# Holding back SyncE's transfers in a block-sparse attention + MLP kernel: each one waits for the landing of the fifth last

## Chip, core and metric

The kernel runs on one core of a Trainium2 chip. The metric is device time in microseconds (us), the median of several executions. Engine names are those of the profile: PE is the matmul engine and PEld its weight loads, DVE is VectorE, ACT is ScalarE, POOL is GpSimd, SP is SyncE, which here does nothing but register arithmetic, waiting and issuing DMA transfers.

## What is computed

```
scores = q @ k^T / sqrt(64)            # 4 batches, 8 heads, 768 positions, fp32
mask: block 32x32; own and neighbour blocks, first and last block row/column,
      and 3 sampled key blocks per query block (given at run time)
attn   = softmax(where(mask, scores, -1e9)) ;  x = attn @ v
x -> 3072 tokens x 512
h = x @ w_in (512 x 2048) ; r = max(h, 0) ; out = (s*r*r + b) @ w_out (2048 x 512)
```

The weights `w_in` and `w_out` come as float64 and are decoded on the chip into two fp32r halves each.

## The kernel before

Two stages share one program. The attention takes the first 260 us or so, the MLP the rest. The attention is cut into "slots": 44 sparse ones (one query block of two batches, all heads; streams A, B and C take turns) and 8 dense ones (first and last block rows). In each sparse slot PE makes the scores (L925), DVE takes the maximum (L942), ACT the exponential (L954), PE transposes (L982), DVE or ACT copies to SBUF (L993, L995), and PE multiplies by the values (L1034, 64 recorded matmuls and 64 weight loads per slot, some from tile `vA`, some from `vB`). Then the result is scaled (L1040), transposed back (L1046), copied by ACT into one of four `xst` buffers (L1051) and written to DRAM (`spill`, L1058 and L1062), from where the MLP reads it (`xload`, L392).

The transfers of the attention and who issues them:

- SP: the keys `kt` (`load_k`, L689 and L692), the queries of dense slots (`load_q`, L706), the three sampled value blocks of each slot (`sampled_v`, L847, three per sparse slot, and L844 for the last block), the whole first window of a stream (`window_v`, L753), the spills, the raw weights of the first `EARLY_W` = 6 weight tiles (`load` in `decode_f64`, L59 and L62), and the loads of x for the MLP's first two groups (L392).
- POOL: the queries of sparse slots (`load_q`, L706) and the next block of each window (`window_v`, L753). POOL also copies keys into `kk` (L864, L875).

The order of the instructions on every engine is written out by a planner (class `Plan`), which runs at build time with a cost for each operation. Its model of SP lets eight transfers be under way:

```
QUEUE = 8
...
sent.append(dma + 850.0)
free[e] = max(free[e], sent[-self.QUEUE])
```

The framework turns the order into queues with semaphores. SP's transfers go through eight landing semaphores in turn, so that a transfer also waits until the eighth last one of SP has landed. An instruction that waits on SP holds up all that stands behind it on SP. The instructions of every engine are themselves brought in by DMA; the profile counts these packets under "instruction".

Of the kernel before, what the change touches and what calls it, by code (L numbers as in the profile page):

```python
# [12 lines left out]
I32 = mybir.dt.int32  # L13
# [23 lines left out]
    return x if x < 2 ** 31 else x - 2 ** 32  # L37


def decode_f64(nc, n, src, top, most, raw_of, mag_of, low_of, hi_of, lo_of):  # L40

    box = {}

    def get(k, fn):
        if k not in box:
            box[k] = fn()  # L50
        return box[k]

    def raw():
        return get("raw", raw_of)

    def load(m=0, parts=1):
        if len(src.shape) == 3:
            a = src.shape[1] // parts
            nc.sync.dma_start(out=raw().rearrange("p (a c) -> p a c", a=src.shape[1])[:, m * a:(m + 1) * a], in_=src.bitcast(I32)[:, m * a:(m + 1) * a])  # L59
        else:  # L60
            a = 2 * n // parts
            nc.sync.dma_start(out=raw()[:, m * a:(m + 1) * a], in_=src.bitcast(I32)[:, m * a:(m + 1) * a])  # L62

    def word(k):
        return raw().rearrange("p (n two) -> p n two", two=2)[:, :, k]

    def mag(t=I32):
        return get("mag", mag_of).bitcast(t)

    def low(t=F32):  # L70
        return get("low", low_of).bitcast(t)

    def hi():
        return get("hi", hi_of)

    A, V = nc.scalar, nc.vector
    return load, [

        ("v", lambda: V.tensor_scalar(out=mag(), in0=word(1), scalar1=0x7FFFFE00, scalar2=None, op0=ALU.bitwise_and), ()),

        ("v", lambda: V.tensor_scalar(out=low(I32), in0=word(1), scalar1=0x1FF, scalar2=None, op0=ALU.bitwise_and), ()),
        ("v", lambda: V.scalar_tensor_tensor(out=low(), in0=low(I32), scalar=2.0 ** 32, in1=word(0).bitcast(U32), op0=ALU.mult, op1=ALU.add), (1,)),  # L82
        ("a", lambda: A.activation(word(1).bitcast(F32), word(1).bitcast(F32), AF.Sign), (0, 1)),

        ("a", lambda: A.activation(mag(F32), mag(), AF.Relu, scale=-8.0, bias=top), (0,)),
        ("a", lambda: A.activation(mag(), mag(F32), AF.Relu, scale=-1.0, bias=most), (4,)),
        ("v", lambda: V.tensor_tensor(out=hi(), in0=mag(F32), in1=word(1).bitcast(F32), op=ALU.mult), (3, 5)),  # L87
        ("v", lambda: V.tensor_scalar(out=mag(), in0=hi().bitcast(I32), scalar1=_i32(0xFF800000), scalar2=None, op0=ALU.bitwise_and), (6,)),  # L88
        ("v", lambda: V.scalar_tensor_tensor(out=lo_of(), in0=low(), scalar=2.0 ** -52, in1=mag(F32), op0=ALU.mult, op1=ALU.mult), (2, 7)),  # L89
    ]  # L90
# [116 lines left out]
def kernel(  # L207
# [16 lines left out]
    nc = tc.nc  # L224
# [4 lines left out]
    NB = 24  # L229
    BLK = 32  # L230
    NPAIR = 4
    NSP = 5
    NSL = 3
# [4 lines left out]
    NM = 12  # L238
    KPS = (4, 24)
    NBC, NCK = 3, 8  # L240
    EARLY_W = 6
# [13 lines left out]
    b_top = cpool.tile([P, 1], F32, name="b_top")  # L255
    nc.gpsimd.memset(b_top, F32_MOST + F64_SHIFT)
    b_most = cpool.tile([P, 1], F32, name="b_most")
    nc.gpsimd.memset(b_most, F32_MOST)
    xd = dpool.tile([B // 2, 2, P, NM, 2, NPAIR, BLK], F32, name="xd")
    wod = dpool.tile([4, P, 2 * DM], F32, name="wod")  # L260

    kp = ctx.enter_context(tc.tile_pool(name="kp", bufs=2))

    def kbig(q, name):
# [2 lines left out]
    NW = NCC * P  # L269
# [103 lines left out]
    def decode(which, f, n):  # L373
        tail = (lambda: scratch("kraw", 2 * NW, f"raw_{which}{f}").bitcast(I32), *parts(n))
        if which == "i":
            src, view = w_in[:, f * P:(f + 1) * P].rearrange("(c p) n -> p c n", p=P), win
        else:
            src, view = w_out[f * P:(f + 1) * P, :], wout
        return decode_f64(nc, NW, src, b_top, b_most, *tail, lambda: view(f, 0), lambda: view(f, 1))


    xsp, xraw, kg_pairs = {}, {}, {}
# [6 lines left out]

    def xload(g, c2, dst=None):  # L390
        t = scratch("kraw", 2 * HALF, f"xraw{g}_{c2}") if dst is None else dst
        nc.sync.dma_start(out=t.rearrange("p (t y) -> p t y", t=NM), in_=xd[g // 4, g % 2, :, :, g // 2 % 2, 2 * c2:2 * c2 + 2, :].rearrange("p t c n -> p t (c n)"))  # L392
        xraw[(g, c2)] = t

    def xsplit(g, c, part=None):
# [259 lines left out]
    with ExitStack() as es:  # L655
# [12 lines left out]
        for w in T["ORD"].split():  # L668
            if w[1] == "D":
                slots.append(("d", "abcd".index(w[0]), int(w[2]), 0))  # L670
            else:
                r = "ABC".index(w[1])
# [8 lines left out]
        kts = {}  # L681


        def load_k(e, a, part):
            if e not in kts:
                kts[e] = kbig(e, f"kt{e}").bitcast(F32)
            rows = slice(part * NB // KPS[e], (part + 1) * NB // KPS[e])
            if a is None:
                nc.sync.dma_start(out=kts[e][:, rows].rearrange("p n a c -> p n (a c)"),  # L689
                                  in_=k_blk[rows, :, 2 * e:2 * e + 2, :].rearrange("n p a c -> p n (a c)"))  # L690
            else:
                nc.sync.dma_start(out=kts[e][:, rows, a], in_=k_blk[rows, :, 2 * e + a, :].rearrange("n p c -> p n c"))  # L692

        qts = {}

# [4 lines left out]
        def load_q(key, a, par):  # L700
            kind, e, t = key
            if key not in qts:
                qts[key] = qp.tile([P, 2, NPAIR, P], F32, tag="qr", name=f"qr{e}_{t}{kind}")
            rows, b = slice(par * D, (par + 1) * D), 2 * e + a
            src = q_dup[b, t, rows, par::2, :] if kind == "s" and t < NSP else q_edge[b, int(kind == "d"), rows, par::2, :]
            (nc.gpsimd if kind == "s" else nc.sync).dma_start(out=qts[key][rows, a], in_=src)  # L706

        vbox = {}

# [5 lines left out]
        def window_values(r):  # L715
            value_tiles()
            return vbox["A"][:, r]
# [16 lines left out]
        def block_rows(e, j, n=1):  # L734

            return v[2 * e:2 * e + 2, j * BLK:(j + n) * BLK, :].rearrange("a r d -> r a d")
# [11 lines left out]
        def window_v(i, entire, m):  # L748

            _, e, k, r = slots[i]  # L750
            rr = [*runs(k, entire), *[(0, NSL, 1)] * entire]
            j, p, n = rr[m]
            (nc.sync if entire else nc.gpsimd).dma_start(out=window_values(r)[p * BLK:(p + n) * BLK], in_=block_rows(e, j, n))  # L753


        ident = pers.tile([P, P], F32, name="ident")
# [18 lines left out]
        box = {}  # L775

        def load_sampled():
            nc.sync.dma_start(
                out=sbi,
                in_=sampled.bitcast(I32).rearrange("a b -> (a b)").rearrange("(o n) -> o n", o=1)  # L780
                .broadcast_to([P, 2 * NB * NSL]))
# [54 lines left out]
        def sampled_v(i, a):  # L836


            _, e, k, r = slots[i]
            row = ring_row("v", i)  # L840
            vt = sampled_values(row)
            if a == 0 and holds["v"].get(row) != e:
                holds["v"][row] = e
                nc.sync.dma_start(out=vt[NSL * BLK:], in_=block_rows(e, NB - 1))  # L844
            src = v[2 * e:2 * e + 2].rearrange("a (n e) d -> n e a d", e=BLK)
            j = block_register(mybir.EngineType.SP, k, r, a)
            nc.sync.dma_start(out=vt[a * BLK:(a + 1) * BLK], in_=src[bass.ds(j, 1)].rearrange("o e a d -> (o e) a d"))  # L847

        def keys_tile():
            if "kk" not in vbox:  # L850
# [202 lines left out]
        def spill(i):  # L1053
            kind, b, k, _ = slots[i]
            xst = xst_of.pop(i)
            if kind == "s":
                hf, m = divmod(k - 1, NM)
                nc.sync.dma_start(out=xd[b, hf, :, m].rearrange("p a c n -> p a (c n)"), in_=xst)  # L1058
                return
            x = k  # L1060
            for m in range(2):
                nc.sync.dma_start(out=xd[b // 2, 1, :, NM - 2 + m, b % 2, 2 * x:2 * x + 2, :],  # L1062
                                  in_=xst.rearrange("p x (a m n) -> p (x a) m n", a=2, m=2)[:, :, m, :])


# [60 lines left out]
        for i, (kind, e, k, r) in enumerate(slots):  # L1126
# [28 lines left out]
            else:  # L1155
                prev = before.get(r)
                entire = k == STREAMS[r]
# [16 lines left out]
                vt = [("vg", "vA"), ("vg", "vB")]  # L1174
                for m in range(len(runs(k, entire)) + entire):
                    n = [*[x for _, _, x in runs(k, entire)], 1][m]
# [8 lines left out]
                lo, n = T["K1"]  # L1185
# [7 lines left out]
            for c in range(2):  # L1193
# [4 lines left out]
                o = op("p", cost[0], u, lambda i=i, c=c: scores(i, c), cols=col[0], deps=deps,  # L1198
                       alloc=banks if new else [], use=[*s_use, *([] if new else banks)])
# [4 lines left out]
            for j in range(nu):  # L1204
                n, ms_ = u + j, []
# [6 lines left out]
                for g in range(ng):  # L1212
                    top = g == 0 and j == 0
# [7 lines left out]
                    else:  # L1221
                        n0, both = n - 1, [half, o_e]
                    o = op("p", 470, u, lambda n=n0, g=g: transposes(n, g), both, cols=1024, alloc=[("B", ("t", n0, g))],
                           use=[("P", (y, g)) for y in range(n0, n + 1)])
# [21 lines left out]
            for j in range(nu):  # L1246
                pts = [("pt", (u + j // 2 * 2, 0))]
                o = op("p", cost[2], u, lambda i=i, j=j: av(i, j), cols=col[2],
                       deps=[*evs[j], *av_deps],
                       alloc=[] if j else [("o", i)],  # L1250
                       use=[*av_use, *pts] + ([("o", i)] if j else []))
# [11 lines left out]
            if k % NBC == 1:  # L1263
                left = sum(sl[0] == "s" and sl[1] == e and sl[2] % NBC == 1 for sl in slots[i + 1:])
                done[e] = done.get(e, 0) + 1
                for b in (2 * e, 2 * e + 1):
                    g = (k - 1) // NBC // (NCK // 2)
# [266 lines left out]
```

## Time and profile before

| | us |
|---|---|
| median of three runs | 784.31 |
| lowest, highest | 782.02, 786.36 |
| profiled execution, device time | 786.43 |
| its span, first to last instruction | 784.7 |
| granted TensorE clock, mean | 0.984 |

The profiled execution is one run, 2.1 us above the median. Its span leaves 1.7 us of the device time outside. Positions in the text ("at 84 us") count from the start of the span. "Landing" is the time from a transfer's issue until its semaphore tells that all data is there. In the chain of work that ended last, "issue" is time in which the engine waited for nothing that the profile shows.

### The profile page before, as it was taken

Reading aid. Unit: us, or ns where it says so; the run is one execution under the profiler, and the core shown is the slowest. Engines: PE = TensorE matmul, PEld = TensorE weight load, DVE = VectorE, ACT = ScalarE, POOL = GpSimd, SP = SyncE. Lnnn points to the kernel's source line nnn. Section 1 sums busy time; section 2 is a strip of 40 time slices with the busy share of each in tenths; the row PEclk is TensorE's granted clock in tenths of the full one; section 3 lists DMA queues with packets and bytes.
Section 4 is the critical chain, followed back from the end, with each engine's and each line's share of the span. In section 5 each row is a group of like instructions: output and inputs, shape, how many; then the busy total and the mean of one; then the engine's idle time right before and its main releaser. Section 6 shows DMA issues by size and latency. Waiting matters only on the chain.

```text
span 784.7 us, 21376 instructions
## 1 busy us (share of the span) xinstructions
PE 734.5 (94%) x8032; PEld 622.3 (79%) x8032; DVE 583.5 (74%) x1436; ACT 472.3 (60%) x1141; POOL 270.4 (34%) x435
## 2 busy tenths in 40 slices
PE   7888689799898999999979999999999999999997
PEld 6566567466566899998768988898999898989996
DVE  3856467788886699998998678687668778666652
ACT  3866466787776687778764334475544467434543
POOL 5836447336641223220423223232232223222321
PEclk9999899999999999999999999999999999999999
DMA  8979689757872444543632421125000022000002
GB/s 249 244 205 239 179 222 252 177 152 197 228 200 88 119 134 142 180 134 119 154 118 66 122 76 61 48 61 162 1 1 1 1 60 82 2 1 0 1 1 80
DMA packets 100167, 89.41 MB, mean 114 GB/s; under 512 B 50464, under 2 KB 79776, under 8 KB 100064
## 3 DMA queue, kind: packets, MB, share of 16 engines
q1 hardware_dynamic: 95936, 76.78, 34.4%
q0 software_dynamic: 4128, 11.28, 5.5%
q8 instruction: 63, 1.03, 0.6%
q14 instruction: 40, 0.33, 0.1%
HBM read 69.15 MB, written 14.68 MB: 107 GB/s over the span
## 4 chain that ended last, share of the span: by engine, by line
PE 65%; DVE 20%; issue 6%; ACT 5%; DMA 2%; SPq 1%; POOL 1%; POOLq 0%; ACTq 0%; DVEq 0%
PE m L611 20%; PE o L475 8%; PE o L476 8%; PE o L474 8%; PE s L925 5%; PE xs L1034 5%; PE t L982 4%; DVE ptile L942 2%; PE od L1024 2%; DVE wkhp L88 2%; PE t L980 2%; PE s L903 1%; PE xs L1046 1%; DVE win L89 1%; DVE wklp L82 1%
## 5 line engine op out<-in xcount | busy, mean ns | idle before, releaser
L453 POOL TENSOR_TENSOR hid<-hid,hid 128x384 fp32r<-128x384 f32 x122 | 134.8, 1106 | 359.6 <-ACT hid L629 261.6
L628 ACT ACTIVATE hid<-hid,sb_b,sb_s 128x384 f32<-128x384 f32 x96 | 68.0, 708 | 151.6 <-DVE hid L622 151.5
L954 ACT ACTIVATE ptile<-ptile,nm 128x256 f32<-128x256 f32 (+1 forms) x208 | 107.0, 517 | 43.2 <-DVE nm L942 43.1
L942 DVE CUSTOM_DVE_ANT_1 ptile<-s,mt 128x256 f32<-128x256 f32 x176 | 64.3, 421 | 29.5 <-PE s L925 28.7
L611 PE MATMUL m<-wout,win 128*128 128x384 f32 x264 | 63.1, 342 | 4.6 <-ACT xrest L1427 4.6
L475 PE MATMUL o<-woutr,hid 128*128 128x512 f32 x168 | 66.4, 396 | 0.7 <-DVE woutr L89 0.7
L476 PE MATMUL o<-woutr,hid 128*128 128x512 f32 x168 | 66.5, 396 | 0.0
L474 PE MATMUL o<-woutr,hid 128*128 128x512 f32 x168 | 65.5, 390 | 0.5 <-DVE woutr L87 0.5
L611 PE MATMUL m<-xp,wop 128*128 128x384 f32 x288 | 58.7, 338 | 0.0
L1034 PEld LDWEIGHTS xs<-vA,pt 128*32 128x32 f32 x1696 | 35.7, 112 | 27.2 <-issue 7.8
L475 PE MATMUL o<-win,hid 128*128 128x512 f32 x144 | 56.8, 394 | 0.0
L622 DVE SCALAR_TENSOR_TENSOR hid<-hid 128x384 f32<-128x384 f32 x96 | 54.0, 563 | 3.3
L611 PE MATMUL m<-xp,win 128*128 128x384 f32 x288 | 54.8, 337 | 1.1 <-DVE sum L1436 0.8
L1034 PE MATMUL xs<-vA,pt 128*32 128x64 f32 x1696 | 47.9, 227 | 7.6 <-issue 3.0
L611 PEld LDWEIGHTS m<-xp,win 128*128 128x128 f32 x288 | 51.0, 188 | 3.7 <-ACT ob L480 1.1
L629 ACT CAST hid<-hid 128x384 fp32r<-128x384 f32 x96 | 49.3, 514 | 7.6 <-ACT hid L628 0.4
L611 PEld LDWEIGHTS m<-wout,win 128*128 128x128 f32 x264 | 48.0, 190 | 7.3 <-ACT xrest L1427 5.5
L611 PEld LDWEIGHTS m<-xp,wop 128*128 128x128 f32 x288 | 52.0, 190 | 2.1
L982 PE MATMUL t<-ident,ptile 128*128 128x128 f32 x352 | 51.6, 290 | 0.9 <-issue 0.8
L875 POOL COPY kk<-kt 128x256 f32 x132 | 50.9, 419 | 0.0
L476 PE MATMUL o<-win,hid 128*128 128x512 f32 x126 | 50.0, 397 | 0.3 <-POOL hid L453 0.3
L621 DVE TENSOR_TENSOR hid<-m,xrest 128x384 f32<-128x384 f32 x48 | 26.5, 551 | 31.0 <-issue 26.4
(184 smaller groups left out, 1867.5 us busy)
## 6 DMA issues: line engine op xcount, KB each, us to landing
vB<-in_v_dram SPq DMA_DIRECT2D x113, 128.0 KB, 4.0
raw_o<-in_w_out_dram SPq DMA_DIRECT2D x14, 512.0 KB, 3.3
raw_i<-in_w_in_dram SPq DMA_DIRECT2D x12, 512.0 KB, 3.8
xd<-xst SPq DMA_DIRECT2D x44, 128.0 KB, 3.9
out_dram<-ob SPq DMA_DIRECT2D x20, 256.0 KB, 2.0
vA<-in_v_dram SPq DMA_DIRECT2D x39, 128.0 KB, 4.1
vA<-in_v_dram POOLq DMA_DIRECT2D x38, 128.0 KB, 3.7
sum<-xd SPq DMA_DIRECT2D x12, 384.0 KB, 4.2
```

What stands on the lines that cost most here:

```text
L453: (eng or nc.vector).tensor_tensor(out=htile(5 + i % 3), in0=t, in1=gh.bitcast(F32), op=ALU.subtract)
L474: nc.tensor.matmul(acc, gh[:, tsl], wout(f, 0), start=first, stop=False)
L475: nc.tensor.matmul(acc, gh[:, tsl], wout(f, 1), start=False, stop=False)
L476: nc.tensor.matmul(acc, gl[:, tsl], wout(f, 0), start=False, stop=last)
L611: nc.tensor.matmul(to, w_, x_, start=(c == 0 and k == 0), stop=(c == 1 and k == 2))
L622: vec.scalar_tensor_tensor(out=t, in0=t, scalar=0.0, in1=t, op0=ALU.max, op1=ALU.mult)
L628: nc.scalar.activation(t, t, AF.Identity, bias=sb_b, scale=sb_s)
L875: nc.gpsimd.tensor_copy(flat(kg[:, a:a + 1]), flat(kts[e][:, bass.ds(j, 1)]))
L942: nc.vector.tensor_tensor_reduce(out=pt, in0=sp, in1=msk, scale=-scale, scalar=FMAX if g == 0 else nm[:, 0:1], op0=ALU.add, op1=ALU.min, a ...
L954: nc.scalar.activation(pt[:, :w], pt[:, :w], AF.Exp, bias=nms[n][:, last:last + 1], scale=-1.0, accum_out=dns[i][:, g, j:j + 1])
L982: nc.tensor.transpose(tp[:, (2 * j + c) * P:(2 * j + c + 1) * P], src[:, c * P:(c + 1) * P], ident)
L1034: nc.tensor.matmul(xs[quads[pair]], pt[:, c, quads[pair]], vt[:, a, col:col + D], start=(j == 0 and c == 0), stop=(c == 1), tile_position= ...
```

## The change

A function `send` takes the place of SP's own issue for the transfers of the attention. It issues the transfer on SP as before, and from the 21st on it adds a dependency: the transfer waits until the fifth last one sent in this way has landed. Which engine issues what, and the planner with its order, stay as they are. POOL's transfers are not held. The raw weights from the seventh tile on, and all later transfers of the MLP, go out as before; so do the two tiny loads of `s` and `b`.

```
+    sent, LEAD, OUT = [], 20, 5
+
+    def send(**kw):
+        ins = nc.sync.dma_start(**kw)
+        if len(sent) >= LEAD:
+            tc.add_manual_dep(ins.ins, sent[-OUT].ins.name, mybir.DependencyInfo(mybir.DependencyClass.Sync, mybir.DependencyReason.DATA))
+        sent.append(ins)
...
-def decode_f64(nc, n, src, top, most, raw_of, mag_of, low_of, hi_of, lo_of):
+def decode_f64(nc, issue, n, src, top, most, raw_of, mag_of, low_of, hi_of, lo_of):
...
-            nc.sync.dma_start(out=raw()[:, m * a:(m + 1) * a], in_=src.bitcast(I32)[:, m * a:(m + 1) * a])
+            issue(out=raw()[:, m * a:(m + 1) * a], in_=src.bitcast(I32)[:, m * a:(m + 1) * a])
...
-        return decode_f64(nc, NW, src, b_top, b_most, *tail, lambda: view(f, 0), lambda: view(f, 1))
+        return decode_f64(nc, send if n < EARLY_W else nc.sync.dma_start, NW, src, b_top, b_most, *tail, lambda: view(f, 0), lambda: view(f, 1))
...
-            (nc.gpsimd if kind == "s" else nc.sync).dma_start(out=qts[key][rows, a], in_=src)
+            (nc.gpsimd.dma_start if kind == "s" else send)(out=qts[key][rows, a], in_=src)
...
-            (nc.sync if entire else nc.gpsimd).dma_start(out=window_values(r)[p * BLK:(p + n) * BLK], in_=block_rows(e, j, n))
+            (send if entire else nc.gpsimd.dma_start)(out=window_values(r)[p * BLK:(p + n) * BLK], in_=block_rows(e, j, n))
...
-            nc.sync.dma_start(out=vt[a * BLK:(a + 1) * BLK], in_=src[bass.ds(j, 1)].rearrange("o e a d -> (o e) a d"))
+            send(out=vt[a * BLK:(a + 1) * BLK], in_=src[bass.ds(j, 1)].rearrange("o e a d -> (o e) a d"))
```

In the same way `nc.sync.dma_start` becomes `send` in `xload` (for the first two groups), `load_k`, `load_sampled`, the L844 load of `sampled_v`, and both forms of `spill`.

## Rows read from the trace of the kernel before

**Rows 1.** The page: span, engines; queue of instructions (packets, MB, share of the engines).
```profile
span 784.7 us, 21376 instructions
...
PE 734.5 (94%) x8032; PEld 622.3 (79%) x8032; DVE 583.5 (74%) x1436; ACT 472.3 (60%) x1141; POOL 270.4 (34%) x435
...
q8 instruction: 63, 1.03, 0.6%
```

**Rows 2.** Chain that ended last: start, us, what; the "issue" pieces.
```profile
34.49 1.16 issue
...
45.36 1.76 issue
...
69.46 0.56 issue
...
74.29 1.52 issue
...
79.69 0.42 issue
...
83.95 5.47 issue
...
129.76 1.03 issue
...
143.07 1.87 issue
```

**Rows 3.** Stretches: length, busy us of PE to POOL, PEclk, DMA share, GB/s.
```profile
66.00:93.00 27.00, 19.03 (x527) 13.82 (x527) 15.06 (x60) 14.73 (x51) 14.35 (x32) 0.88 0.83 224
75.81:79.69 3.88, 3.88 (x127) 2.93 (x127) 2.11 (x7) 1.73 (x7) 2.75 (x6) 1.00 1.02 255
80.12:83.95 3.83, 3.83 (x127) 2.87 (x126) 3.11 (x13) 2.76 (x10) 3.12 (x8) 1.00 0.88 241
```

**Rows 4.** SP's L847, L1058, L689, then POOL's L753, L706, from 66 to 88 us.
```profile
L847 SPq DMA_DIRECT2D vB<-in_v_dram x10: 316/330/1123, 66.6 to 79.8; - x10
...
L847 SPq DMA_DIRECT2D vA<-in_v_dram x3: 342/342/484, 81.4 to 83.1; - x3
...
DMA to landing us min/median/max: 4.5/6.3/7.9
...
L1058 SPq DMA_DIRECT2D xd<-xst x5: 349/364/373, 65.7 to 82.5; - x5
...
L689 SPq DMA_DIRECT2D kt<-in_k_blk_dram x9: 334/422/1528, 67.0 to 86.1; - x9
...
L753 POOL DMA_DIRECT2D vA<-in_v_dram x6: 536/550/550, 67.4 to 84.3; - x6
...
L706 POOL DMA_DIRECT2D qr_3s<-in_q_dup_dram x4: 615/623/629, 69.1 to 73.1; - x4
```

**Rows 5.** Landing of L847's transfers, first from 40 to 66 us, then 118 to 147.
```profile
DMA to landing us min/median/max: 2.1/3.7/5.9
...
DMA to landing us min/median/max: 2.4/5.1/6.4
```

**Rows 6.** Stretches as in 3: after the longest stop, 118 to 150, after the attention.
```profile
89.42:93.20 3.78, 3.78 (x42) 2.86 (x50) 1.37 (x4) 0.86 (x2) 0.00 (x0) 0.50 0.05 16
118.00:150.00 32.00, 28.58 (x613) 20.31 (x615) 24.29 (x85) 21.91 (x67) 16.56 (x37) 0.96 0.91 235
262.00:385.00 123.00, 120.72 (x602) 108.34 (x601) 113.33 (x188) 96.95 (x175) 27.25 (x24) 1.00 0.49 146
```

**Rows 7.** L1034's matmuls up to 110.35 us; then L847's transfers up to 100.2 us.
```profile
L1034 PE MATMUL xs<-vA,pt x640: 216/219/244, 30.2 to 108.0; 128*32 128x64 f32 x160
...
L1034 PE MATMUL xs<-vB,pt x384: 216/219/316, 38.7 to 103.3; 128*32 128x64 f32 x192
...
L847 SPq DMA_DIRECT2D vB<-in_v_dram x41: 316/326/1179, 21.4 to 100.1; - x41
...
L847 SPq DMA_DIRECT2D vA<-in_v_dram x12: 316/340/484, 15.7 to 83.1; - x12
```

More of the change, by code (lines that the diff above doesn't have):

```diff
@@ L58, in load @@
             a = src.shape[1] // parts
-            nc.sync.dma_start(out=raw().rearrange("p (a c) -> p a c", a=src.shape[1])[:, m * a:(m + 1) * a], in_=src.bitcast(I32)[:, m * a:(m + 1) * a])
+            issue(out=raw().rearrange("p (a c) -> p a c", a=src.shape[1])[:, m * a:(m + 1) * a], in_=src.bitcast(I32)[:, m * a:(m + 1) * a])
         else:
             a = 2 * n // parts
-            nc.sync.dma_start(out=raw()[:, m * a:(m + 1) * a], in_=src.bitcast(I32)[:, m * a:(m + 1) * a])
+            issue(out=raw()[:, m * a:(m + 1) * a], in_=src.bitcast(I32)[:, m * a:(m + 1) * a])
     def word(k):
@@ L391, in xload @@
         t = scratch("kraw", 2 * HALF, f"xraw{g}_{c2}") if dst is None else dst
-        nc.sync.dma_start(out=t.rearrange("p (t y) -> p t y", t=NM), in_=xd[g // 4, g % 2, :, :, g // 2 % 2, 2 * c2:2 * c2 + 2, :].rearrange("p t c n -> p t (c n)"))
+        (send if g < 2 and dst is None else nc.sync.dma_start)(out=t.rearrange("p (t y) -> p t y", t=NM), in_=xd[g // 4, g % 2, :, :, g // 2 % 2, 2 * c2:2 * c2 + 2, :].rearrange("p t c n -> p t (c n)"))
         xraw[(g, c2)] = t
@@ L688, in load_k @@
             if a is None:
-                nc.sync.dma_start(out=kts[e][:, rows].rearrange("p n a c -> p n (a c)"),
+                send(out=kts[e][:, rows].rearrange("p n a c -> p n (a c)"),
                                   in_=k_blk[rows, :, 2 * e:2 * e + 2, :].rearrange("n p a c -> p n (a c)"))
             else:
-                nc.sync.dma_start(out=kts[e][:, rows, a], in_=k_blk[rows, :, 2 * e + a, :].rearrange("n p c -> p n c"))
+                send(out=kts[e][:, rows, a], in_=k_blk[rows, :, 2 * e + a, :].rearrange("n p c -> p n c"))
         qts = {}
@@ L777, in load_sampled @@
         def load_sampled():
-            nc.sync.dma_start(
+            send(
                 out=sbi,
@@ L843, in sampled_v @@
                 holds["v"][row] = e
-                nc.sync.dma_start(out=vt[NSL * BLK:], in_=block_rows(e, NB - 1))
+                send(out=vt[NSL * BLK:], in_=block_rows(e, NB - 1))
             src = v[2 * e:2 * e + 2].rearrange("a (n e) d -> n e a d", e=BLK)
             j = block_register(mybir.EngineType.SP, k, r, a)
-            nc.sync.dma_start(out=vt[a * BLK:(a + 1) * BLK], in_=src[bass.ds(j, 1)].rearrange("o e a d -> (o e) a d"))
+            send(out=vt[a * BLK:(a + 1) * BLK], in_=src[bass.ds(j, 1)].rearrange("o e a d -> (o e) a d"))
         def keys_tile():
@@ L1057, in spill @@
                 hf, m = divmod(k - 1, NM)
-                nc.sync.dma_start(out=xd[b, hf, :, m].rearrange("p a c n -> p a (c n)"), in_=xst)
+                send(out=xd[b, hf, :, m].rearrange("p a c n -> p a (c n)"), in_=xst)
                 return
@@ L1061, in spill @@
             for m in range(2):
-                nc.sync.dma_start(out=xd[b // 2, 1, :, NM - 2 + m, b % 2, 2 * x:2 * x + 2, :],
+                send(out=xd[b // 2, 1, :, NM - 2 + m, b % 2, 2 * x:2 * x + 2, :],
                                   in_=xst.rearrange("p x (a m n) -> p (x a) m n", a=2, m=2)[:, :, m, :])
```

## The prediction

> **What bounds the kernel now.** I read the page first. PE is busy 94% of the span [rows 1], so only a change that gives PE time back, or takes some, moves the end. The second view is the chain of work that ended last, cut to the attention, the only part that the diff touches. Most of its pieces are PE's, but between them stand pieces called "issue", in which PE waits for nothing that the profile shows: eight of them, from 0.42 to 5.47 us, in [rows 2], 13.8 us in sum. What are they? The stretches between two of them answer it. From the end of the piece at 74.29 to the next, and from there to the one after, PE ran 127 matmuls and 126 or 127 weight loads each time [rows 3], wherever in a block of work that ended (the stop at 83.95 is between two matmuls of L1034). The page has 63 packets of instructions on one queue, 1.03 MB, so 16.4 KB each, and PE has 8032 + 8032 instructions [rows 1], 255 for each packet. So PE stops where one packet of its own instructions is used up and the next is not there: an instruction fetch, which is a DMA, comes late.
>
> The third view is the landing of the data transfers in the same stretch. From 66 to 88 us SP's L847 takes 6.3 us in the median to land [rows 4], from 40 to 66 us 3.7 us [rows 5], and the DMA engines are 83% busy [rows 3]. PE uses up a packet in 3.8 to 3.9 us [rows 3]. A fetch that lands as late as the data beside it then holds PE. The four stops from 66 to 93 us (0.56, 1.52, 0.42, 5.47) sum to 7.97 us, just the 27.00 - 19.03 us in which PE is idle there [rows 2, 3].
>
> **How deep SP's queue is.** Transfers under way are their number times their landing time over the stretch. From 66 to 88 us SP issues 13 of L847, 5 of L1058 and 9 of L689, 27 in 22 us [rows 4]; with 6.3 us for each (the one median shown) that is 7.7 under way, about the eight that the framework allows. POOL issues 6 of L753 and two groups of four of L706 (one of the two is shown) [rows 4], 14; with the same landing, 4.0 under way. So the rule of five binds here, and takes 11.7 under way to 9.0. From 40 to 66 us SP's L847 lands in 3.7 us, and the rule binds in bursts only.
>
> **The change part by part.**
>
> *The wait itself* is SP's alone. Behind a waiting transfer stand the next transfers with their register arithmetic, and the spills. For them wait PE (sampled values), POOL (keys) and ACT (a free `xst`, of which there are four). What covers the delay is that sampled values come early. The first 16 sparse slots are 16 x 64 = 1024 matmuls of L1034, and these (640 + 384) had run by 110.35 us. The 17th slot needs 51 transfers of L847; 53 had been issued by 100.2 us [rows 7]. Even with the longest landing of [rows 4], 7.9 us, the data is there by 108.1 us, 2.3 us ahead; worked out in the same way from each slot's own landing, the slack of all 44 slots is 8.3 us (this one) or more. Cost taken: 0. If the cover is gone, each us beyond it is a us of PE's.
>
> *Does the rule slow the flow of data?* With 4.9 us to land (below), five under way are 1.02 transfers per us, and 27 in 22 us are 1.23. The flow of SP would be 17% lower, and in a 22 us burst the last transfer 22 x (1.23/1.02 - 1) = 4.5 us late, less than the 8.3 us. If instead the DMA engines, 83% busy, stay as busy, POOL's transfers and the fetches just go first and nothing is late. Bounds: 0 and 4.5 us of delay, all under the slack; I take 0 for PE.
>
> *Earlier fetches.* If landing follows the number under way, it falls by 1 - 9.0/11.7 = 23%: from 6.3 to 4.9 us, 1.4 us less. If only SP's own queue counts, by 1 - 5/7.7 = 35%, 2.2 us less. From 66 to 93 us the stops of 0.56 and 0.42 go, and 1.52 and 5.47 lose 1.4 each: 3.8 us (with 2.2 us: 4.7). From 118 to 150 us L847 lands in 5.1 us [rows 5], 23% are 1.2 us: 1.03 goes, 1.87 loses 1.2, 2.2 us. The stop at 34.49 loses 0.9, 23% of the 3.7 us of the stretch behind it. The one at 45.36 stands where landing is short, and keeps its 1.76. Sum 6.9 us.
>
> Not all of it reaches the end. From 66 to 93 us the chain holds PE and "issue" alone, so 3.8 counts in full. From 118 to 150 us DVE is busy 24.3 of 32 us [rows 6] and shares the chain; I count half of 2.2, and half of 0.9 at 34.49: 1.5. From 5.3 I take 0.8 off, since a fetch that now falls outside a burst may then fall into one (a 1.76 us stop with short landings shows that chance has a part). **Value: 4.5 us**, between 0 (fetches do not follow the queue) and 6.9, with 4.7 in place of 3.8 some 8 us.
>
> *The clock.* After the stop of 5.47 us PE ran at 0.50 of its clock (1.2 in place of 2.4 GHz) from 89.42 to 93.20, 3.78 us of work [rows 6] that takes 1.9 us at full clock. If the stop gets short enough, 1.9 us more come back. At 4.1 us it would still be the longest of all; I take 0, and put 1.9 into the range.
>
> *What the gain meets later.* After the attention DVE decodes weights and PE runs the MLP, with DVE busy 113 and PE 121 of 123 us [rows 6]: full engines that start as much earlier as the attention ends earlier. Nothing of the diff acts there, since the loads from the seventh weight tile on are not held.
>
> **Sum.** 786.43 - 4.5 = 781.9 us for the profiled execution, which is 2.1 us above the median of 784.31. Off the median: 779.8 us, 0.57% less. About 0.5% (3.9 us) is what a measurement of this kernel can tell from no change.
>
> **Rivals.**
>
> *No change to be seen (784 us).* A fetch on its own queue may not care how many of SP's transfers wait in theirs. For it: the stop of 1.76 us at 45.36 in a stretch of short landings, and stops of 0.42 and 5.47 us one after the other in the same deep burst. Against it: three quarters of the stops in [rows 2] by time lie where landing takes 5.1 to 6.3 us. A smaller effect of the same kind, 0 to 3.9 us, ends here too: 780.4 to 788.2, most likely 783. The Trainium skill would have it so twice: "DMA: Bandwidth & Descriptors" (Queues, rings and completion order) says that a DMA engine serves its queues in turn, packet by packet, so that a fetch waits for a packet or so of each other queue; "Runtime: NRT & Kernel Launch" (Instruction fetch mechanics) says that instructions come in 16 KiB blocks of 256, mostly hidden. The block size agrees with this trace (16.4 KB for 255); "mostly hidden" does not in the attention, where one stop is 5.47 us; by either rule the sum would be 784.3.
>
> *Slower: SP starves PE.* If landing stays at 6.3 us though only five are under way (a slow DMA engine sets it, not the queue), the flow is 0.79 per us against 1.23, and a 22 us burst ends 22 x (1.23/0.79 - 1) = 12 us late. It decides from 8.3 us of delay on: PE then waits some 4 us, and as much again in the burst from 118 to 150 us: 784 + 8 = 792 us. Against it: landing of 3.7 us where fewer are under way, so landing does follow the queue. A smaller form, late spills that leave ACT no `xst`, would be of the order of the bound.
>
> *Much faster.* If SP's queue alone sets the fetch and the clock holds: 8 + 1.9, 774 us.
>
> **Chances.** Faster by 3 to 7 us 0.50 (of which 0.08 is less than 3.9 us); much faster 0.08; no change 0.32; slower by more than 3.9 us 0.10. So faster 0.50, same 0.40, slower 0.10. The range goes from 774 us, the much faster case, to 787, which leaves out the slower case and little more.
>
> **What would show it.** Right: in the chain from 66 to 93 us the "issue" piece of 5.47 us is 4 us or less, the sum of the four is about 4, and L847 lands in about 4.9 us there; POOL's landings fall too; the attention's last spill is 4 to 5 us earlier; stretches behind it keep their length. Wrong: PE waits for `vA`, `vB` or `kk` in the waits by a DMA or POOL; ACT waits for spills; or the "issue" pieces stay as they are though fewer transfers are under way, or turn up at other packets with the same sum.

## The result, and the profile after

The change made the kernel slower: 791.2 us in the median of eight runs (787.6 to 792.5) against 783.3 for eight of the kernel before (781.2 to 787.1), a ratio of 1.0094 with an interval of 1.0071 to 1.0116. The forecast was 779.8.

The two profiled executions differ by less, since that of before (786.43 us) lies near the upper end of its runs and that of after (787.58) is the fastest of its own. Both kernels were therefore profiled once more (779.7 and 793.8 us). Where the second pair differs, its numbers are given beside those of the first. In the kernel after, all held transfers of SP bear one line, L267 (`send`); the other lines of the attention are those of before plus 8 (L1034 is L1042, L1051 is L1059).

The page of after, to set beside [rows 1]: span, engines, queue of instructions.

```profile
span 785.8 us, 21379 instructions
...
PE 736.1 (94%) x8032; PEld 622.5 (79%) x8032; DVE 582.6 (74%) x1436; ACT 471.9 (60%) x1141; POOL 269.4 (34%) x435
...
q8 instruction: 63, 1.03, 0.6%
```

The work and its packets of instructions are the same. The page tells nothing of the loss; the stretches do. Those of after, with the columns of [rows 3]:

```profile
66.00:93.00 27.00, 23.69 (x766) 17.73 (x752) 19.01 (x81) 18.61 (x65) 16.38 (x38) 1.00 0.84 230
...
118.00:150.00 32.00, 22.99 (x429) 15.19 (x428) 19.09 (x66) 15.26 (x46) 11.95 (x28) 0.88 0.74 221
...
262.00:385.00 123.00, 120.99 (x602) 108.17 (x601) 113.60 (x188) 97.06 (x174) 27.45 (x25) 1.00 0.48 145
```

From 66 to 93 us PE now does 766 matmuls instead of 527 [rows 3]: time is won. From 118 to 150 us it does 429 instead of 613, and DVE, ACT and the DMA engines all do less too [rows 6]: more time is lost. From 262 us on the stretch is what it was.

**Where it was won.** The chain's "issue" pieces of after from 66 to 93 us, beside the four of [rows 2] (0.56, 1.52, 0.42 and 5.47):

```profile
73.85 1.25 issue
...
82.69 2.06 issue
```

The same stretch in the second profile of before:

```profile
67.05 0.28 issue
...
71.61 1.80 issue
...
77.29 1.25 issue
...
82.36 3.00 issue
```

The sums are 7.97 and 6.33 us without the rule, 3.31 and (second profile of after) 3.85 with it. The longest stop fell from 5.47 to 2.06 us in the first pair, but in the second it was 3.00 before and 2.99 after: how long one stop is differs from run to run. Landing fell with the stops. SP's transfers from 66 to 88 us by kind (KB each, median us to landing), before:

```profile
vB<-in_v_dram SPq DMA_DIRECT2D x10, 128.0 KB, 6.0
kt<-in_k_blk_dram SPq DMA_DIRECT2D x9, 128.0 KB, 6.0
xd<-xst SPq DMA_DIRECT2D x5, 128.0 KB, 5.9
vA<-in_v_dram SPq DMA_DIRECT2D x3, 128.0 KB, 7.7
```

and after, where the median of all is 4.0:

```profile
vB<-in_v_dram SPq DMA_DIRECT2D x9, 128.0 KB, 4.5
kt<-in_k_blk_dram SPq DMA_DIRECT2D x7, 128.0 KB, 3.8
xd<-xst SPq DMA_DIRECT2D x4, 128.0 KB, 4.0
vA<-in_v_dram SPq DMA_DIRECT2D x1, 128.0 KB, 4.0
...
DMA to landing us min/median/max: 2.4/4.0/6.3
```

Landing is shorter for every kind, but 21 transfers were issued where before had 27, and the DMA engines had less to do. The same 22 us as a stretch (columns of [rows 3]), before and then after:

```profile
66.00:88.00 22.00, 15.44 (x488) 11.15 (x480) 13.69 (x56) 13.95 (x49) 14.35 (x32) 0.96 0.98 263
...
66.00:88.00 22.00, 18.69 (x606) 13.69 (x594) 15.49 (x65) 15.05 (x53) 14.78 (x34) 1.00 0.86 236
```

In the second pair the share of the DMA engines is 0.96 before and 0.80 after.

**Where it was lost.** After's chain from 118 to 150 us: start, us, what.

```profile
124.96 2.97 DMA xd<-xst
...
127.96 4.78 DMA raw_i<-in_w_in_dram
132.75 4.24 DMA vB<-in_v_dram
...
137.38 4.25 DMA raw_o<-in_w_out_dram
...
142.80 5.11 DMA vA<-in_v_dram
...
147.99 1.88 DMA xd<-xst
...
149.96 0.27 ACT xst L1059
```

For 25 us the chain is a relay: a transfer lands, SP issues the next one that waited for it, that one lands, and so on, until the last landing, a spill's, gives ACT an `xst` to write. Before's chain has no relay there: between 100 and 155 us it has one piece of DMA, 4.55 us (4.52 in its second profile). The second profile of after has the same relay (2.92, 5.20, 4.76, 3.71, 4.29 and 2.54 us). What the engines wait for, up to 262 us, after: engine, its line, what it waited for, us, times, longest.

```profile
ACT xst L1059 <- DMA xd<-xst: 7.3, 2, 4.7
...
DVE wkhp L79 <- DMA raw_i<-in_w_in_dram: 5.1, 1, 5.1
...
POOL vA L761 <- DMA vB<-in_v_dram: 4.7, 1, 4.7
...
PE xs L1042 <- DMA vB<-in_v_dram: 2.8, 1, 2.8
```

and before:

```profile
PE xs L1034 <- DMA vA<-in_v_dram: 2.6, 1, 2.6
...
ACT xst L1051 <- DMA xd<-xst: 1.7, 1, 1.7
```

The waits for landings cost clock as well. Behind the wait of 2.41 us for `vB` at 104.35, ahead of the relay, PE's granted clock was 0.56 on the mean from 107.84 to 111.62 (most of it at 1.2 in place of 2.4 GHz), and one block of 32 matmuls of L933 took 1.91 us there, 1.02 us at full clock. Behind the relay it was 0.50 from 150.78 to 154.55.

A common yardstick for all runs is the time at which PE reaches one and the same instruction. This table is counted from the traces (nr. 3523 and nr. 6339 of PE's matmuls, weight loads and semaphore instructions; both are first in a packet):

```
us from the start of the span       3523rd   6339th   between
before                               95.07   160.58     65.5
before, second profile               90.85   156.49     65.6
after                                88.70   165.48     76.8
after, second profile                90.61   169.09     78.5
```

Between the two instructions the change loses 11.3 us in the first pair and 12.9 in the second. What is left of the span behind the second one differs by some us from run to run (624.1 and 621.4 us before, 620.3 and 622.9 after).

SP issues the same 396 transfers in the same order in both kernels, so that its delay can be read transfer by transfer (counted from the traces, start in us):

```
SP's transfer                                   before   after   later    second pair, later
61st, keys                                        50.9    57.2     6.3         5.7
103rd, a sampled block                            83.1    95.4    12.2        14.5
115th, last sampled block of the 17th slot        98.8   104.4     5.6        10.9
145th, a raw weight of the relay                 120.0   128.0     7.9        13.6
168th, the spill that ends the relay             138.7   148.0     9.3        17.0
```

### The profile page after: what moved, and what is told of

Read it like the earlier page. It is cut to its first block, busy times and chain, and to the rows that moved or that the text cites. A ratio compares the mean times of both kernels' runs of the same rounds, so it can differ in the third digit from the quotient of the medians.

```text
span 785.8 us, 21379 instructions
## 1 busy us (share of the span) xinstructions
PE 736.1 (94%) x8032; PEld 622.5 (79%) x8032; DVE 582.6 (74%) x1436; ACT 471.9 (60%) x1141; POOL 269.4 (34%) x435
## 4 chain that ended last, share of the span: by engine, by line
PE 64%; DVE 19%; ACT 6%; DMA 5%; issue 4%; SPq 1%; ACTq 0%; DVEq 0%
PE m L619 20%; PE o L483 8%; PE o L484 8%; PE o L482 8%; PE s L933 6%; PE xs L1042 5%; PE t L990 5%; PE od L1032 2%; DVE wkhp L88 2%; DVE ptile L950 2%; DVE win L89 1%; PE xs L1054 1%; DVE wklp L82 1%; PE t L988 1%; SPq L267 1%
## 5 line engine op out<-in xcount | busy, mean ns | idle before, releaser
L1042 PEld LDWEIGHTS xs<-vA,pt 128*32 128x32 f32 x1696 | 35.6, 113 | 23.1 <-ACT xst L1059 8.9
L1042 PE MATMUL xs<-vA,pt 128*32 128x64 f32 x1696 | 48.0, 227 | 2.9 <-DVE nm L950 0.9
L990 PEld LDWEIGHTS t<-ident,ptile 128*128 128x128 f32 x352 | 38.7, 144 | 14.0 <-ACT ptile L962 6.3
```

Of the source, the lines that this page charges most:

```text
L990: nc.tensor.transpose(tp[:, (2 * j + c) * P:(2 * j + c + 1) * P], src[:, c * P:(c + 1) * P], ident)
L1042: nc.tensor.matmul(xs[quads[pair]], pt[:, c, quads[pair]], vt[:, a, col:col + D], start=(j == 0 and c == 0), stop=(c == 1), tile_position= ...
```

## The experiments

The expectations weigh two readings of the loss. The *order* reading: single transfers that are needed at once (spills, raw weights) stand in SP's order behind others that have much slack. The *flow* reading, later called the lag: SP carries fewer transfers per us all through the attention, and falls behind whatever it is that comes next.

**Part of the sends held.** First the 21st to the 103rd alone, then those from the 104th on.

```
-        if len(sent) >= LEAD:
+        if LEAD <= len(sent) < 103:      # held early
...
+        if len(sent) >= 103:             # held late
```

> The rule holds only SP's 21st to 103rd attention transfers, which end at about 95 us; all later ones go out as before the change. Order theory (the rule helps PE's instruction fetches, and loses only between 95 and 157 us, where spills and raw weights, which ACT and DVE need soon, queue on SP behind transfers that nobody needs soon): the gain up to 95 us stays (6.4 us at the same matmul in the two profiles) and the loss goes, so 775 to 779 us against 783, ratio 0.99 to 0.995. Flow theory (holding slows the data everywhere and the earlier fetches buy nothing in the end): 783 us or more, ratio 1.00 or above.

Measured: 785.8 us, 1.0028 (1.0003 to 1.0052). The early part alone is not the gain that the order reading wanted, but a small loss.

> The complement: the first 103 of SP's attention transfers go out unheld, the later ones are held. Order theory: the long fetch stop near 84 us is back (5 us) and the loss after 95 us stays (11 us in the two profiles between 95 and 157 us, of which some 4 came back later): 790 to 796 us, ratio about 1.01 to 1.015. Flow theory: the loss is shared between both parts, 785 to 788 us.

Measured: 787.1 us, 1.0058 (1.0036 to 1.0080), where the flow reading had it. The two halves add up to 0.86 of the 0.94%, each with an uncertainty of 0.2 or more. No single stretch carries the loss. Nor does the loss need a delay from before 95 us: with the late part alone held, 0.58% was lost.

**Raw weights free.** The early raw weights go out on SP without the rule, the rest is held.

```
-        return decode_f64(nc, send if n < EARLY_W else nc.sync.dma_start, NW, ...
+        return decode_f64(nc, nc.sync.dma_start, NW, ...
```

> All as changed, but the raw weights of the first six tiles go out without the rule (they still stand in SP's order, and are not counted among the five). Order theory: they are late mainly because of what stands before them, so only part of DVE's wait for them (5.1 us in the changed profile) goes: 787 to 790 us, against 791 for the change. Rival: the rule on these large transfers is the whole loss (each of 256 KB keeps a place of the five for about 5 us), then 783 us or less.

Measured: 789.3 us, 1.0100 (1.0061 to 1.0138), nothing regained: a raw weight that need not wait itself still stands behind transfers that do. DVE still waited 4.0 us at L79, where it reads its first raw weight, and ACT's waits for `xst` were 6.8 us.

**Depth of the rule**: seven, six and four under way.

```
-    sent, LEAD, OUT = [], 20, 5
+    sent, LEAD, OUT = [], 20, 7      # then 6, then 4
```

> The seventh last in place of the fifth last. Order theory: some 6.7 under way in the deep bursts instead of 7.7, so the fetches gain a little and the held transfers lose a little: within 3 us of before, 781 to 786 us, ratio 0.997 to 1.003. If the wait instruction itself or the dependency costs something whatever the depth: 788 us or more.

> Six under way instead of five. Theory of the lag: the flow lies between that of five and seven, so does the time: 784 to 788 us, ratio 1.001 to 1.006, and SP has issued 93 to 101 transfers by 85 us. Rival, a cost that comes with each wait whatever its depth: 790 to 792 us as with five, although seven cost nothing.

> Four under way instead of five. Theory of the lag: SP's flow from 20 to 85 us falls from 1.05 to about 0.9 transfers per us, so some 78 issued by 85 us, and the loss at least doubles: 800 to 815 us, ratio 1.02 to 1.04. Rival, a cost that comes with each wait whatever its depth: 790 to 793 us. Rival, the landing falls with the number under way and the flow stays: 788 to 792 us.

Measured: seven 782.2 us, 0.9987 (0.9961 to 1.0014); six 784.2 us, 1.0019 (0.9993 to 1.0045); four 801.3 us, 1.0213 (1.0152 to 1.0274). A fixed cost of each wait (790 us or so at six) is out, and so is a flow that stays as it is (788 to 792 us at four). In the table, SP's issues are the sum over the groups of the issues from 20 to 85 us; the stops are PE's idle time in front of the first instruction of a packet that had landed less than 1.75 us before, summed over the attention (from the trace).

```
under way        ratio    SP issues    ACT waits     stops at
                          20 to 85 us  for xst, us   packets, us
as before        1           84           1.7 (2.3)  17.9 (again 14.2)
seven            0.9987      83           4.5        10.3
six              1.0019      79           5.1        12.5
five             1.0094      71           7.3 (7.8)  7.3 (again 10.7)
four             1.0213      64          18.3         4.1
```

In brackets: the second profile. The fewer under way, the further SP is behind, and the longer ACT waits. The stops are longest without the rule and shortest with four; seven, six and five cannot be put in order, since five alone gives 7.3 and 10.7. That the packets themselves come earlier, and not only PE later, shows in the time from PE's start on one packet to the moment when the next begins to be brought: 2.5 and 2.4 us on the mean of the first 24 without the rule, 1.7 and 1.8 with five, 1.5 with four (counted from the traces). The groups of issues of before, from 20 to 85 us (KB each, median us to landing):

```profile
vB<-in_v_dram SPq DMA_DIRECT2D x40, 128.0 KB, 4.8
kt<-in_k_blk_dram SPq DMA_DIRECT2D x17, 128.0 KB, 5.2
vA<-in_v_dram SPq DMA_DIRECT2D x12, 128.0 KB, 3.9
xd<-xst SPq DMA_DIRECT2D x11, 128.0 KB, 4.1
```

and of after, where besides these four groups, as before, four single transfers make up the sum:

```profile
vB<-in_v_dram SPq DMA_DIRECT2D x36, 128.0 KB, 4.1
kt<-in_k_blk_dram SPq DMA_DIRECT2D x12, 128.0 KB, 3.8
vA<-in_v_dram SPq DMA_DIRECT2D x11, 128.0 KB, 4.0
xd<-xst SPq DMA_DIRECT2D x8, 128.0 KB, 3.7
```

**The two kernels once more**, one profile each.

> The kernel before once more, for a second profile of it. The first profile came from its slowest side (786.4 us, median 783). If that draw made the stops for instructions look larger than they usually are, the sum of the eight stops, 13.8 us in the first profile, is 8 to 11 us here and the attention ends 2 to 4 us earlier. If it was typical, the stops near 75 to 84 us are again 7 to 8 us in sum and the end of the attention stays within 1 us.

> The changed kernel once more, for a second profile; the first came from its fastest side (787.6 us, median 791). Order theory: ACT waits again for spills to land (7.3 us in the first profile, 1.7 us before the change) and DVE for raw weights (5.1 us, none before), both between 95 and 160 us, with 6 to 16 us in sum. Chance: these waits are gone here and others stand in their place.

Measured: 779.7 and 793.8 us; their rows are above. At the eight packets of [rows 2] PE stops 10.3 us in the second profile of before, 3.00 instead of 5.47 at the longest, and the 6339th instruction comes 4.1 us earlier: part of the 13.8 us was the draw of one run. In the second profile of after ACT waits 7.8 us for spills and DVE 6.0 us for raw weights, as the order reading wanted.

**The deep burst alone held.**

```
-        if len(sent) >= LEAD:
+        if 77 <= len(sent) < 104:
```

> The rule holds only SP's 78th to 104th transfers, those of the burst from about 66 to 85 us; before and behind it SP is as free as in the kernel before. Theory that the loss is a lag which SP gathers over the whole attention (about 15 transfers by 85 us under the whole rule): SP enters the burst with the lead of the kernel before (about 80 issued by 66 us), loses at most 8 transfers of it by 85 us, and wins them back unheld; most of the fetch gain of about 4 us stays: 778 to 783 us, ratio 0.994 to 1.000, and the 13th fetch boundary lies near 90 us. Rival, the hold in the deep burst alone starves PE, whatever lead SP brings: as with the rule up to the 103rd transfer, 785 to 788 us, ratio about 1.003.

Measured: 785.1 us, 1.0011 (0.9983 to 1.0040). This does not tell the two apart. SP had 98 transfers out at 85 us where before has 104, as the lag wants, but the gain did not show; the profiled run (779.9) was the fastest of twelve. It reached the 3523rd instruction at 92.62 us.

**Spills on ACT's queue**, under the rule and (there from `nc.sync.dma_start`) without it.

```
-                send(out=xd[b, hf, :, m].rearrange("p a c n -> p a (c n)"), in_=xst)
+                nc.scalar.dma_start(out=xd[b, hf, :, m].rearrange("p a c n -> p a (c n)"), in_=xst)
...
-                send(out=xd[b // 2, 1, :, NM - 2 + m, b % 2, 2 * x:2 * x + 2, :],
+                nc.scalar.dma_start(out=xd[b // 2, 1, :, NM - 2 + m, b % 2, 2 * x:2 * x + 2, :],
```

> The changed kernel, with the spills issued by ACT instead of SP, unheld: ACT has just written the buffer, and no spill stands behind SP's held transfers any more. To be read against the kernel before with the same move (e5). Order theory by way of the spills: most of the change's loss of 8 us goes, so this is within 3 us of e5. If the spills do not matter (the loss is in the raw weights or in the flow): 6 us or more above e5.

> The kernel before, with the spills issued by ACT. The issue costs ACT some 0.35 us for each of 60 transfers, by SP's own rows, of which the attention's end sees what ACT has not idle: 0 to 6 us; the 1.7 us that ACT waits for a spill go. 781 to 789 us.

Measured: 798.5 us, 1.0222 (1.0183 to 1.0261) with the rule, 800.4 us, 1.0227 (1.0195 to 1.0259) without. The rule costs nothing in this pair; but both are 15 and 17 us slower than the kernel before and wait 7.9 and 10.4 us for `raw_i`, so that a loss may be hidden behind it. Why the move to ACT costs so much was not traced.

**Release of `xst` taken away.** The spills keep their place on SP, their size and their wait for ACT's copy, but read a constant tile, so that x does not reach the MLP; one of the four `xst` buffers makes room for it.

```
-            xst = xst_of.pop(i)
+            xst = xz[:, :xst_of.pop(i).shape[1], :]
...
-                send(out=xd[b, hf, :, m]..., in_=xst)
+                after_copy(send(out=xd[b, hf, :, m]..., in_=xst), i)   # waits for copy i
```

> The rule of five as in the change; the spills keep their place, their bytes and their wait for ACT's copy, but they read a constant tile, so ACT never waits for a spill to give its xst buffer back. What they write is not x, so the MLP works on constants; its time does not depend on the values. Theory that the late spills are the main price (ACT without xst: 7.3 us of waits under the rule, 1.7 without it): most of the loss goes, 781 to 786 us, within 0.4% of the pair kernel without the rule. Rival, SP's lag as such is the price and whatever stands late next takes over (raw weights, value blocks, keys): 788 to 792 us, 0.6 to 1.0% over the pair kernel, with the waits for raw_i, vA and vB as long as or longer than with the rule alone.

> The pair kernel: the kernel before with the same constant source for the spills, no rule. Both theories: ACT's waits for xst sum to only 1.7 us there, so 780 to 785 us, ratio 0.996 to 1.002.

Measured: with the rule 782.9 us, 1.0023 (0.9999 to 1.0046), without it 782.0 us, 0.9991 (0.9959 to 1.0024). The rule now costs 0.3 points (0.9 us) instead of 0.9 (7.9 us). The two intervals overlap, so that these 0.3 cannot be told from nothing; that they are less than the 0.9 is clear of noise (from the single runs, a mean cost of 1.5 us with some 2 us either way, against 6.8 with 2). So the late spills, by way of ACT's free `xst`, are the greater part of the net loss. They are not all that SP's delay costs: with the rule DVE waits 6.9 us for raw weights and POOL 4.4,

```profile
DVE wkhp L79 <- DMA raw_i<-in_w_in_dram: 6.9, 1, 6.9
...
POOL vA L762 <- DMA vB<-in_v_dram: 4.4, 1, 4.4
...
PE xs L1043 <- DMA vA<-in_v_dram: 3.2, 1, 3.2
```

while the pair kernel without it has only

```profile
PE xs L1034 <- DMA vA<-in_v_dram: 2.6, 1, 2.6
```

of these. By the yardstick, the 3523rd instruction is reached at 89.3 us with the rule and 95.0 without, and from there to the 6339th it is 71.6 against 64.1 us: 7.5 us lost where the change loses 11 to 13. What the other waits cost and what the fetches gain nearly cancel.

## Why the prediction was wrong

**What bounds the kernel: right.** The stops are at packet boundaries, and they get shorter with fewer transfers under way. They fell from 14 to 18 us over the attention to 7 to 11 with five and 4 with four; the four profiles without the rule (before twice, and the two experiments on spills) have 14.2 to 17.9, the five that hold all or nearly all sends by five 7.3 to 11.1 (counted in the same way). The rival by which a fetch does not care for the queue is out. The Trainium skill, "DMA: Bandwidth & Descriptors" (Queues, rings and completion order), has each DMA engine serve its queues in turn by packets; what the prediction drew from that, an unchanged fetch, did not come about here. Two readings were off. The chain had more such pieces than eight (one of 0.75 us at 55.41; by packets the attention has 14 stops), and the share of 83% for the DMA engines is that of 66 to 93 us, the long stop's idle end included: in the 22 us of the burst it was 0.98.

**The earlier fetches: right in size, in part by luck.** Up to the 3523rd instruction the forecast is 3.8 us and half of 0.9, some 4.2; the 4.5 is for the whole attention. Five kernels hold the early sends by five with everything before the 3523rd instruction as in the change or nearly so: after twice, raw weights free, early part held and the last pair's first reach it at 88.70, 90.61, 88.75, 91.63 and 89.26 us, on the mean 89.8. Four without an early rule (before twice, held late, and the last pair's second) reach it at 95.07, 90.85, 95.44 and 95.02, on the mean 94.1. That is 4.3 us, from one profile each, and the two groups overlap (91.63 and 90.85). At the eight packets of [rows 2] PE stops 13.8 and 10.3 us before, 4.5 and 6.5 after (counted from the traces): 6.5 us less on the mean, where the forecast's sum was 6.9; but the two near 130 and 144 us are at nothing there in a stretch in which PE waits for data. Stop by stop the forecast did not hold: the one at 34.49, expected to lose 0.9, was 1.21 at 36.18 in after and 2.69 in its second profile, and the longest was 3 us in both kernels of the second pair. The sampled values' landing fell further than the 4.9 us forecast, to 4.5 for `vB`. The clock, taken as 0, gave something back in the first pair: behind its longest stop PE ran at 1.00 from 84.75 to 89.00, where before had 0.50 [rows 6]; in the second pair it was 0.63 before and 0.59 after.

**The price of the wait, "Cost taken: 0": wrong, and this step turned the sign.** Two things failed in it.

The lag was worked out for one burst of 22 us, 4.5 us, with the rule binding "in bursts only" before it. But the rule binds from the 21st transfer on: the 61st goes out 6.3 us later, and the 103rd 12.2 us (14.5 in the second pair), more than the 8.3 us of slack that the text itself named as the point from which it counts. From 20 to 85 us SP issues 71 instead of 84, 15% fewer; the predicted 17% was nearly right as a rate, and was counted over too short a time. SP's waits show what reserve it had. Before, 20 to 95 us (line, what SP waited for, us, times, longest):

```profile
SPq L1058 <- ACT xst L1051: 8.6, 4, 6.0
SPq L847 <- PE xs L1034: 4.2, 4, 1.5
SPq L689 <- DMA vB<-in_v_dram: 2.8, 2, 1.9
```

after:

```profile
SPq L267 <- DMA vA<-in_v_dram: 6.6, 7, 2.9
SPq L267 <- DMA vB<-in_v_dram: 5.1, 9, 1.2
SPq L267 <- DMA kt<-in_k_blk_dram: 3.1, 5, 1.5
SPq L267 <- ACT ptile L962: 2.2, 3, 1.2
...
SPq L267 <- DMA xd<-xst: 1.3, 2, 1.2
...
SPq L267 <- PE xs L1042: 0.3, 2, 0.2
```

Before, SP stood 12.8 us for ACT's copies and for the buffers that PE's L1034 reads: there it was early. In the second profile of before the same two lines are only 5.5 us, and the longest single wait, 6.0 and 3.4 us, stands beside PE's longest stop (5.47 and 3.00 us), so that part of it is ACT's copies coming late themselves. Under the rule SP stands 16.1 us for landings, 2.2 for ACT and 0.3 for PE's L1042 (second profile 18.2, 3.1 and 1.7). So SP had 5 to 13 us to give, where the rule makes the 103rd transfer 12 to 14 us later. From 95 to 150 us before's SP waits 0.4 us for `xst` and 3.7 for PE, so that little is made up there.

And the slack was read against PE as it was before, and for the sampled values only, with 8.3 us or more in all 44 slots. The first slot for whose data PE waited in after was the very one that it named, the 17th. In the first pair its last block lands 4.7 us later (106.76 instead of 102.08), about the delay that was forecast; but PE comes to the slot 6.6 us earlier (103.76 instead of 110.40), about what it had won by then, and the two together are more than 8.3: PE waits 2.8 us. What the change gains at PE is taken from the same slack. In the second pair PE comes there no earlier, and the landing alone, 10.8 us later, is enough for a wait of 1.3 us. The dearer waits were those which the prediction named ("for them wait PE, POOL and ACT") and for which it worked out no slack: ACT's free `xst` (7.3 us) and DVE's raw weights (5.1).

**The slower rival: right in its price, and that is partly luck.** It gave 792 us and a burst that ends 12 us late, but from a landing that stays at 6.3 us, and with PE as the one that waits. Landing fell, SP was late all the same, and the greater part came by way of ACT: 21 transfers in 22 us at 4.0 us are 3.8 under way, less than the five allowed. That the fifth last must land, and not any five, and that SP issues in order, may be why; no run tested it. The "smaller form, late spills that leave ACT no `xst`" was the larger one, and had been put at "the order of the bound".

**What stays open.** Of the 11 to 13 us lost between the two instructions of the yardstick, the release of `xst` accounts for some 4 to 5 (11 to 13 less 7.5). How the other 7.5 divide into raw weights, keys and value blocks was not tried one by one; the run with free raw weights shows only that releasing them alone helps nothing. Both figures rest on one profile of each kernel of the pair. No version beat the kernel before: seven under way, at 0.9987, cannot be told from it.

## What to carry to other kernels

A queue that issues in order hands a delay on to all that stands in it. Where the order stays the same, read the delay transfer by transfer, and compare it with the slack of each consumer, summed over all the time in which the new wait binds; then look for the consumer with the least slack, not the one with the most traffic. Take from that slack what the change gains at the consumer: who comes earlier needs its data earlier. When a limit shortens landing, count the transfers issued per us as well: here, from 66 to 88 us, landing got 25 to 37% shorter for the three commonest kinds and SP still issued 22% fewer.

## What the runs showed of the hardware

That PE's instruction fetches depend on the data transfers under way was not expected to show so clearly between the extremes: 18 or 14 us of stops without the rule, 11 or 7 with five, 4 with four (10 and 13 with seven and six, in no order). Nor that a limit lowers landing and flow together: from 66 to 88 us, where the DMA engines were busy 0.98 of the time, five under way brought landing from 6.0 to 4.5 us (`vB`) and the engines' share to 0.86.
